# Sliding-window attention with sinks into a four-expert mixture: gates by token, first weights in pieces, score bursts joined

## The chip, the core and the metric

One core of one Trainium2 chip runs the whole kernel in one launch. The metric is device time in microseconds (us) of that core. TensorE (PE in the profile) has a matmul stream and a weight-load stream (PEld) beside it; VectorE (DVE), ScalarE (ACT), GpSimd (POOL) and SyncE (SP) have a queue of their own each. GpSimd and SyncE here issue nearly all DMAs. The inputs lie in DRAM in fp32; the load through GpSimd's DMA turns them into bf16 on the way.

## The reference

```python
# attention: q, k, v are (B, H, S, D) = (4, 8, 768, 64); 4 sink keys, window 128
scores = (q @ k.T) / sqrt(D)
keep   = (key_pos < 4) | ((0 <= q_pos - k_pos) & (q_pos - k_pos < 128))
a      = softmax(where(keep, scores, -1e9))
x      = (a @ v) with heads side by side            # (3072 tokens, 512)
# mixture: 4 experts, w1 (512, 1024), w2 (1024, 512)
p   = domain_probs / (domain_probs.sum(-1) + 1e-9)  # (3072, 4), the gates
out = sum over e of p[:, e] * (relu(x @ w1[e]) @ w2[e])
```

Every token goes through all four experts, so the mixture is by far the larger part of the arithmetic. The output is fp32, 3072 x 512.

## The kernel before

**Tiles.** Tokens are taken in twelve groups of 256, three to a batch: group (b, g). A unit (b, g, e) is the first product of one group with one expert. It leaves H = relu(x w1), as bf16, in two layouts: plain (eight blocks of 128 hidden columns) or as the parts that the second product needs.

**Attention, for each batch.** Rows of q and k are turned so that the 64 elements of a head lie on partitions: on TensorE for batch 0 (L579), by a transposing DMA in SyncE's queue for the batches after (L247). Then, for each of four head pairs and each group, scores of two heads are computed at once on 64 rows each (L685), ScalarE takes the exponential (L710), VectorE multiplies by the window's mask (L704, L719; for the first group of batch 0 a bias matmul, L679, takes its place), the four sink keys are treated beside that (L646, L654), the values are multiplied (L744, L751), VectorE takes the reciprocal of the row sums (L778) and the result is scaled (L781, L790). The result is turned to x by TensorE in batch 0 (L809) and by SyncE's transposing DMA after that (L768). A run of score matmuls between other matmuls is called a burst here: one head pair has six matmuls, and two head pairs in one burst have twelve. `Attention.options` (L849) says which steps could come next; `Attention.two` (L844) says whether the next two score steps may be joined.

**Mixture.** Units before `START[e]` are plain: eight blocks of four matmuls of 256 columns into a bank each (L1071). All others use a seven-product (Strassen-like) form on 2x2 blocks: products P1 to P7 (L1158) of forms of w1 (`weight_form1`, made on VectorE, L364 to L383) with forms of the tokens (L1127); ScalarE and VectorE add parts between banks (L1204, L1211, L1217, L1226), and VectorE applies relu and the gate together (L1191). The second products of the first two groups (`NEARLY`) are plain: eight matmuls of 512 columns into one of two banks `acc` (L1423), scaled by the gate `scale_t` and summed over the experts by VectorE (L1433, L1435), and stored (L1441). The ten other groups again use seven products, each summed over the four experts (L1335), copied out by ScalarE (L1375, L1397), added by VectorE (L1381, L1386) and stored by SyncE (L1324, L1383). These ten share one buffer `osb`.

**Gates.** The probabilities `dp` lie in SyncE's first loads as 24 rows of 128 tokens. They are needed in two ways. `gates_by_row` (L431) normalises them in this layout, writes them to DRAM, and `load_gate` (L452) loads one row to all partitions for the seven-product units. `gates` (L918), called just ahead of the first plain second product, turns `dp` on TensorE (four fp32 matmuls of 24 rows, L921), normalises on VectorE (L923 to L926) and leaves `scale_t`, 128 x 24 x 4, of which the plain second products use the first four tiles of 128 tokens.

**Loads.** GpSimd's queue loads q, k, v and the weights. `load_w1` (L308) loads w1 of an expert in `parts` pieces of columns; before the change expert 0 comes in two halves (L492, L493), the others in one piece, each w2 in one. The first loads stand in the code in order; the later ones come from a list `loads` (L1459 to L1461, extended in the main loop).

**What sets the order.** The instruction streams come from a planner that runs while the program is built. It keeps an estimated clock for each engine and DMA path (`t`, L103) and cost functions (`pe`, `act`, `dve`, `pool`, `sp`, `lands`), a ring of six PSUM banks, and a list of evictions to come (`later`, `flush`). At each turn of the main loop (L1481 to L1563) it collects what could be issued on TensorE next: steps of attention, a first product of an open unit, the opening of a new unit, a plain second product, one of the seven second products. Each has a ready time and a priority (`DUE`, `LOW_PRODUCT`, `OPEN` and so on; lower goes first). Among those ready within 40 ns the lowest priority number is taken, else the one ready first. Attention counts as due when it is behind its share of the mixture's work (`SHARE_OF`); a batch's attention may begin when the mixture has done a part (`LEAD`) of the work of the batches before. Where nothing is ready in the first 20 us by the planner's clock, `idle_products` (L555) issues matmuls on zeros. Weight forms are made when `form_due` and its counterpart for w1 say so (L388 to L398).

Of the kernel before, what the change touches and what calls it, by code (L numbers as in the profile page):

```python
# [10 lines left out]
AX = mybir.AxisListType  # L11
FP32 = mybir.dt.float32
# [4 lines left out]
def kernel(  # L17
# [12 lines left out]
    nc = tc.nc  # L30
# [7 lines left out]
    P = 128  # L38
# [22 lines left out]
    FIRST = 1  # L61
    START = {0: (1, 0), 1: (0, 2), 2: (0, 0), 3: (1, 0)}
    MIX = 6
    SHARE_OF = (0.91, 0.78, 1.08)
    LEAD = (1.01, 0.90)
    DUE = 1.5
    LOW_PRODUCT = 2.7
    LOW_SECOND = 2.7
    HIGH_PRODUCT = 1.9
    EARLY = -0.01  # L70
    MASK = 4000
    GATE = 1500
    GATE0 = 500
    FORM = 6000
    TOKEN = 5000
    MARGIN = 500
    HOLD = 0
    FULL = 7
    STEP0 = 0.01
    READY = 40  # L80
    WIDE = 2
    OPEN = 2.2
    SOON = 21000
    NEARLY = 2
    ROWED = 24000
    GATED = 38000
# [1 line left out]
    ROWS1 = 1500  # L88
    ONACT = 1
    ONE = 2  # L90
    PAIR = 1
    BEHIND = 1500
    CHORES = 3
    BIASED = 1
# [8 lines left out]
    t = {"pe": 1200.0, "act": 0.0, "dve": 0.0, "pool": 1280.0, "sp": 800.0, "sw": 6500.0, "hw": 0.0}  # L103
    ring, whole = [0.0] * 6, [False] * 6
    WARM = 6600.0
    FLIP, LATE, SLOW = 300, 2500, 1500

    def pe(cols, *deps, n=1, switch=0):
        t["pe"] = max([t["pe"], *deps])
        rate = 2.4 if t["pe"] > WARM else 1.2  # L110
        t["pe"] += cols / rate + 2.5 * n + 95 * switch
        return t["pe"] + 215
# [16 lines left out]
    def free_at(n=1):  # L129

        return sorted(ring)[n - 1]
# [51 lines left out]
        return act(cols) if engine == "act" else dve(cols, rate=rate, fixed=fixed)  # L183

    landed = {}
    ROW = {64: 12.8, 128: 22.6, 512: 79.8, 1024: 156.2}

    def lands(key, rows, cols, *deps):
        issued = pool(0, *deps, fixed=880)
# [118 lines left out]
    def load_w1(e, parts=1, which=None):  # L308
        if e not in w1_sb:
            w1_sb[e] = wpool.tile([P, NDB, F], BF16, name=f"w1_{e}", tag=f"w1_{e}")  # L310
        n = F // parts
        for i in which or range(parts):
            nc.gpsimd.dma_start(
                out=w1_sb[e][:, :, i * n:(i + 1) * n],
                in_=moe_w1[e][:, i * n:(i + 1) * n].rearrange("(db p) f -> p db f", p=P),
            )
# [71 lines left out]
    def form1_due(e):  # L388
        n = formed1.get(e, 0)
        if e == E - 2 and not (loaded and out_sb):  # L390
            return False
        return landed.get(("w1", e), 1e12) + 4000 < t["pe"] and (n < 3 or n == 3 and not left1[e])

    def form_due(e):
        n = formed.get(e, 0)
        if e == E - 1 and spared_at.get("w2", 1e12) > t["pe"]:
            return False
        return landed.get(("w2", e), 1e12) + 9000 < t["pe"] and (n < 3 or n == 3 and e in used)  # L398

    forming = []  # L400

# [94 lines left out]
    landed["w1", 0, 1] += 300  # L496
    landed["w1", 0] += 300
    load_w2(0)
    for base, sgn in ((0, 1), (NSINK - 1, -1)):
# [225 lines left out]
    def scores_ready(b, hp, g, n=1):  # L725
        return max([free_at(2 * n)] + [x for i in range(n) for x in turned(b, g, hp + i)])
# [98 lines left out]
    class Attention:  # L825
# [16 lines left out]
            return bool(self.todo or self.scored or self.valued)  # L842

        def two(self):  # L844
            return self.b >= PAIR and len(self.scored) <= 2 and len(self.todo) > 1 and self.todo[0][::3] == self.todo[1][::3] and self.todo[0][0] == "scores"

        def flip_ready(self):
            _, b, g, hp = self.flips[0]
# [3 lines left out]
        def options(self):  # L852

            if self.valued:
                yield turn_ready(*self.valued[0]), "turn"
            if self.scored and len(self.valued) < 3:
                yield values_ready(*self.scored[0]), "values"
            if self.todo:
                kind, b, x, y = self.todo[0]
                if kind == "scores":  # L860
                    if len(self.scored) < 4:
                        yield scores_ready(b, x, y), "todo"
                    if self.two():
                        yield scores_ready(b, x, y, 2), "two"
                elif kind == "keys":
                    yield max(turned(b, 0)), "todo"
                elif kind == "sinks":
                    nxt = self.todo[1] if len(self.todo) > 1 else None
                    if b >= 1 and nxt and nxt[0] == "scores":
                        if len(self.scored) < 4:  # L870
                            yield max(sinks_ready(b, x, y), scores_ready(*nxt[1:]), free_at(3)), "both"
                    else:
                        yield sinks_ready(b, x, y), "todo"
            if self.flips:
                yield self.flip_ready() + (FLIP if self.b == 0 and self.flips[0][2] else 0), "flip"
# [37 lines left out]
                    sink_values(b)  # L913


    scale_t = consts.tile([P, NT, E], FP32, name="scale_t")

    def gates():  # L918
        pt = acc[1][:, 0:E * NT].rearrange("p (e t) -> p e t", e=E)
        for e in range(E):  # L920
            nc.tensor.transpose(pt[:, e], dp[:, :, e], identf[0:NT, 0:NT])  # L921
# [4 lines left out]
        nc.vector.tensor_mul(  # L926
            scale_t, pt.rearrange("p e t -> p t e"), rs[:, :, None].to_broadcast([P, NT, E]),
        )
        acc_free[1] = dve(600, pe(400, acc_free[1]))

    NH = 6
    QF = NFB // 2
# [5 lines left out]
    class Mixture:  # L938
# [63 lines left out]
        def unit_ready(self, b, g, e, first):  # L1002
# [10 lines left out]
        def early_ready(self, g):  # L1013
            if not self.early[g] or not self.room():
                return 1e12
            return max(t["pe"], self.unit_ready(0, g, self.early[g][0], True))

        def firsts(self):

            early = sum(map(len, self.early.values()))  # L1020
            zero = sum(u["unit"] < PAIRS[0] for u in self.open)
            n = len(self.open)
            for i, u in enumerate(self.open):
                b, g, e = u["unit"]
                if u["fast"]:
                    for m in u["left"]:
                        yield max(u["at"].get(m, 1e12), free_at() if m == "P5" else 0.0), 2 + STEP0 * i, (u, m)
                else:
                    j = u["left"][0]
                    yield self.unit_ready(b, g, e, j < QF // 2), 2 + STEP0 * i, (u, j)  # L1030
            if n < WIDE and early:
                at, g = self.next_early()
                yield at, (OPEN if n else 2), ("early", g)
            if n < WIDE and self.units and (self.units[0][0] or loaded) and early <= MIX and self.room() and not (early + zero and self.live >= NH - 1):
                yield self.unit_ready(*self.units[0], False), (OPEN if n else 2) - EARLY, ("unit",)

        def emit_first(self, what, ready):

# [442 lines left out]
    while mix.more() or att.more():  # L1481
# [54 lines left out]
        opts += [(max(f, now), p, "first", x) for f, p, x in mix.firsts()]  # L1536
# [62 lines left out]
```

## Time and profile before

| | us |
|---|---|
| median of three timed runs | 359.38 (358.82, 359.38, 360.85) |
| the profiled execution's own time | 359.66 |
| its span in the trace | 358.0 |
| PE busy, matmuls | 351.3 |
| PEld busy, weight loads | 302.8 |
| DVE busy | 305.9 |
| ACT busy | 165.5 |
| POOL busy | 71.6 |

The span runs from the first to the last recorded instruction; the execution's own time has 1.66 us around it. Busy times of different engines overlap, and matmul ends are modelled, so a busy PE is not PE at its peak. The profile's page cuts the span into 40 equal slices and gives each engine's busy tenths in each:

```profile
PE   8999999999999999999998999999999999999996
DVE  6787979986999999798798899899889799899840
...
PEclk9999999999999999999999999999999999999999
DMA  9999999999999999617299812010220132111011
```

TensorE's line is at nine tenths or more except at both ends and in one slice of the middle; the granted clock is full throughout; the DMA engines are busy for the first 16 slices, in which q, k, v of the first batches, all weights and the first gates come in, and mostly idle later.

### The profile page before, as it was taken

How to read it: one execution, taken by the hardware profiler on the slowest of the kernel's cores; microseconds unless marked ns; L12 is line 12 of the kernel's file. 1: busy time of each engine (PE TensorE's matmuls, PEld its weight loads, DVE VectorE, ACT ScalarE, POOL GpSimd, SP SyncE). 2: the span in 40 equal slices, each digit the busy share in tenths (PEclk: the TensorE clock that was granted, in tenths of full speed). 3: DMA queues.
4: the chain of work that ended last, by engine and by line, in shares of the span. 5: the costliest groups of instructions: out<-in, count | busy, mean ns of one | idle time of the engine just before them, and what ended most of it. 6: DMA issues, size and time to landing. Idle time of an engine off the chain costs nothing.

```text
span 358.0 us, 10896 instructions
## 1 busy us (share of the span) xinstructions
PE 351.3 (98%) x4568; PEld 302.8 (85%) x4568; DVE 305.9 (85%) x698; ACT 165.5 (46%) x424; POOL 71.6 (20%) x92
## 2 busy tenths in 40 slices
PE   8999999999999999999998999999999999999996
PEld 4585769756789988989998898999899999999985
DVE  6787979986999999798798899899889799899840
ACT  5764623448782564556543445345444422313111
POOL 8945115230626106001061000000000000000000
PEclk9999999999999999999999999999999999999999
DMA  9999999999999999617299812010220132111011
GB/s 172 180 188 200 221 218 181 164 150 183 157 130 155 126 174 132 86 60 76 31 158 166 140 58 60 33 60 21 56 75 17 32 75 60 31 42 35 1 60 60
DMA packets 118013, 37.79 MB, mean 106 GB/s; under 512 B 100692, under 2 KB 113460, under 8 KB 117964
## 3 DMA queue, kind: packets, MB, share of 16 engines
q0 software_dynamic: 77520, 17.31, 56.5%
q1 hardware_dynamic: 39388, 19.28, 28.8%
q8 instruction: 35, 0.57, 0.7%
q10 hardware_dynamic: 1056, 0.52, 0.5%
q14 instruction: 14, 0.11, 0.1%
HBM read 40.98 MB, written 6.34 MB: 132 GB/s over the span
## 4 chain that ended last, share of the span: by engine, by line
PE 91%; DMA 4%; ACT 2%; POOL 1%; DVE 1%; issue 0%; SPq 0%; ACTq 0%
PE cps L1158 35%; PE acc L1335 33%; PE hps L1071 8%; PE acc L1423 7%; PE sps L685 3%; PE od L751 3%; DMA out_dram<-osb 2%; DMA qkn<-in_k_dram 2%; PE od L744 1%; ACT aT L710 1%; POOL qkn L235 1%; POOL vx L300 1%; PE tr L579 0%; DVE osb L1433 0%; PE tx L809 0%
## 5 line engine op out<-in xcount | busy, mean ns | idle before, releaser
L1158 PEld LDWEIGHTS <-w 128*128 128x128 bf16 x1280 | 78.5, 98 | 2.7 <-issue 1.3
L1335 PEld LDWEIGHTS <-H 128*128 128x128 bf16 x708 | 65.2, 98 | 7.5 <-issue 1.3
L1191 DVE SCALAR_TENSOR_TENSOR H<-cps,gates 128x512 bf16<-128x512 f32 x99 | 66.3, 681 | 1.5 <-PE cps L1158 1.3
L1158 PEld LDWEIGHTS <-vf 128*128 128x128 bf16 x960 | 58.6, 98 | 1.7 <-issue 0.8
L710 ACT ACTIVATE aT<-sps 128x512 bf16<-128x512 f32 (+1 forms) x96 | 47.6, 572 | 23.5 <-PE sps L685 23.4
L1335 PE MATMUL acc<-w,H 128*128 128x256 bf16 x420 | 55.4, 273 | 0.0
L1158 PE MATMUL cps<-T,w 128*128 128x128 bf16 x640 | 48.7, 219 | 0.0
L1158 PE MATMUL cps<-xT,w 128*128 128x128 bf16 x640 | 48.2, 219 | 0.0
L1158 PE MATMUL cps<-T,vf 128*128 128x128 bf16 x640 | 46.7, 219 | 0.0
L1204 ACT COPY cps<-cps 128x512 f32<-128x512 f32 x40 | 23.2, 581 | 44.1 <-PE cps L1158 32.7
L790 ACT ACTIVATE onat<-od,R 128x64 bf16<-128x64 f32 x144 | 33.5, 336 | 18.0 <-DVE R L778 18.0
L1211 DVE TENSOR_TENSOR cps<-H,cps 128x512 f32<-128x512 f32 x35 | 24.2, 691 | 12.5 <-PE cps L1158 10.6
L1335 PEld LDWEIGHTS <-S 128*128 128x128 bf16 x320 | 30.1, 98 | 4.6 <-issue 1.6
L1397 ACT COPY osb<-acc 128x256 f32<-128x256 f32 x35 | 13.1, 377 | 41.7 <-PE acc L1335 38.7
L300 POOL DMA_DIRECT2D vx<-in_v_dram x24 | 21.4, 897 | 53.5 <-PE od L751 43.0
L1071 PE MATMUL hps<-xT,w 128*128 128x256 bf16 x256 | 31.3, 273 | 0.0
L1423 PE MATMUL acc<-w,H 128*128 128x512 bf16 x128 | 30.1, 379 | 0.0
L1335 PE MATMUL acc<-wf,H 128*128 128x256 bf16 (+1 forms) x208 | 28.4, 272 | 0.0
L1071 PEld LDWEIGHTS <-w 128*128 128x128 bf16 x256 | 24.3, 98 | 4.2 <-issue 0.3
L1226 DVE TENSOR_TENSOR H<-H,cps 128x512 f32<-128x512 f32 x35 | 23.8, 681 | 2.8 <-PE cps L1158 2.6
L1158 PE MATMUL cps<-xT,vf 128*128 128x128 bf16 x320 | 24.4, 219 | 0.0
L704 DVE TENSOR_TENSOR aT<-aT,mask 128x1024 bf16<-128x1024 bf16 (+1 forms) x36 | 22.8, 637 | 1.3 <-ACT aT L710 1.2
(127 smaller groups left out, 516.7 us busy)
## 6 DMA issues: line engine op xcount, KB each, us to landing
w<-in_moe_w_dram POOLq DMA_DIRECT2D x7, 1024.0 KB, 16.8
out_dram<-osb SPq DMA_DIRECT2D x21, 256.0 KB
gates<-gate_rows SPq DMA_DIRECT2D x40, 128.0 KB
vx<-in_v_dram POOLq DMA_DIRECT2D x24, 128.0 KB, 6.7
qkn<-in_q_dram POOLq DMA_DIRECT2D x22, 128.0 KB, 8.0
qkn<-in_k_dram POOLq DMA_DIRECT2D x22, 128.0 KB, 10.5
w<-in_moe_w_dram POOLq DMA_DIRECT2D x2, 512.0 KB, 9.0
kraw<-in_k_dram ACTq DMA_DIRECT2D x2, 256.0 KB
```

The costliest lines, as they stand in the source:

```text
L300: nc.gpsimd.dma_start(out=vx[tb][:, :, 0:D], in_=v[b, :, tb * P:(tb + 1) * P, :].rearrange("h p d -> p h d"),)
L704: nc.vector.tensor_mul(a, a, m[:, None, :].to_broadcast([P, 2, w]))
L710: nc.scalar.activation(out=a[:, ph], in_=sps[ph][:, 0:w], func=AF.Exp, scale=scale)
L790: nc.scalar.mul(o[:, qi, hp, ph * D:(ph + 1) * D], od[:, qi, ph, 0:D], R[:, qi, ph])
L1071: nc.tensor.matmul(h[:, i].rearrange("p (q n) -> p q n", q=2), lhsT=w1_sb[e][:, db, fb * P:(fb + 1) * P], rhs=xT[b, g][:, :, db], start=(i ...
L1158: nc.tensor.matmul(y[:, f], lhsT=A[:, d, f * P:(f + 1) * P], rhs=T[:, d], start=(m in ("P1", "P5") and f == 0 and d == 0), stop=(d == 1), ...
L1191: nc.vector.scalar_tensor_tensor(out=dst, in0=src, scalar=0.0, in1=gate, op0=ALU.max, op1=ALU.mult)
L1204: nc.scalar.copy(out=tiles["Y"], in_=y)
L1211: nc.vector.tensor_add(tiles["V"], c5, tiles["X"])
L1226: nc.vector.tensor_add(c5, c5, y)
L1335: nc.tensor.matmul(y, lhsT=self.operand(b, g, e, m)[:, f], rhs=forms[e][m][:, f, cs], start=(k == 0 and f == 0 and m in (("P1", "P5", "P2" ...
L1423: nc.tensor.matmul(op, lhsT=H[:, fb // QF, fb % QF, s], rhs=w2_sb[e][:, fb, :], start=(fb == 0), stop=(fb == NFB - 1),)
```

## The change

**Gates by token.** `scale_t` is now 128 x 4 x 4 and is loaded by a DMA of SyncE, tokens on partitions, right after the loads of the sink values; a piece of it is four fp32 numbers. `gates` only normalises it in place on VectorE: no matmuls, and the first plain second product does not wait for the bank that they used.

**First weights in pieces.** w1 of expert 0 is loaded by four DMAs of 256 columns instead of two of 512, w1 of expert 1 by two instead of one. `unit_ready` looks up the landing of the piece that a product uses, where it knew the first half and the whole before. The planner's assumed landings change with that.

**Single bursts wait for joined ones.** Where the next two score steps could be joined, the single one is now called "one" instead of "todo" and gets a priority number of at least `DUE + ALONE`, unless attention is late by more than `OVER` steps or the batch is the first. While a joined burst is possible, due and not late, and at least `HOLDS` units are open, `joins` keeps new units from being opened. With `PAIR = 0` joined bursts are allowed in batch 0, too.

**Order refitted.** Twelve of the planner's constants have other values, so that the order changes from the start to the end of every queue.

```diff
-    SHARE_OF = (0.91, 0.78, 1.08)
-    LEAD = (1.01, 0.90)
-    DUE = 1.5
-    LOW_PRODUCT = 2.7
+    SHARE_OF = (0.9, 0.79, 0.98)
+    LEAD = (1.01, 1.0)
+    DUE = 1.9
+    LOW_PRODUCT = 2.3
...
-    GATE0 = 500
+    GATE0 = 900
...
-    MARGIN = 500
+    MARGIN = 0
...
-    SOON = 21000
+    SOON = 34000
...
-    PAIR = 1
+    HOLDS = 1
+    MORE = 2
+    BOTH = 1
+    PAIR = 0
+    OVER = 4
+    ALONE = 1.3
...
-    FLIP, LATE, SLOW = 300, 2500, 1500
+    FLIP, LATE, SLOW = 500, 2900, 1500
...
-        return landed.get(("w1", e), 1e12) + 4000 < t["pe"] and (n < 3 or n == 3 and not left1[e])
+        return landed.get(("w1", e), 1e12) + 3000 < t["pe"] and (n < 3 or n == 3 and not left1[e])
...
-        return landed.get(("w2", e), 1e12) + 9000 < t["pe"] and (n < 3 or n == 3 and e in used)
+        return landed.get(("w2", e), 1e12) + 14000 < t["pe"] and (n < 3 or n == 3 and e in used)
...
+    scale_t = consts.tile([P, 2 * NEARLY, E], FP32, name="scale_t")
+    nc.sync.dma_start(out=scale_t, in_=moe_domain_probs[0:2 * NEARLY * P].rearrange("(t p) e -> p t e", p=P))
...
-    load_w1(0, 2, [0])
-    load_w1(0, 2, [1])
+    load_w1(0, 4, [0])
+    load_w1(0, 4, [1])
+    load_w1(0, 4, [2])
+    load_w1(0, 4, [3])
...
-                        yield scores_ready(b, x, y), "todo"
+                        yield scores_ready(b, x, y), "one" if self.two() else "todo"
...
-        pt = acc[1][:, 0:E * NT].rearrange("p (e t) -> p e t", e=E)
-        for e in range(E):
-            nc.tensor.transpose(pt[:, e], dp[:, :, e], identf[0:NT, 0:NT])
-        rs = consts.tile([P, NT], FP32, name="rs")
-        nc.vector.reduce_sum(out=rs, in_=pt.rearrange("p e t -> p t e"), axis=AX.X)
+        rs = consts.tile([P, 2 * NEARLY], FP32, name="rs")
+        nc.vector.reduce_sum(out=rs, in_=scale_t, axis=AX.X)
...
-            return max(free_at(), landed.get(("w1", e, 0), 1e12) if first else landed.get(("w1", e), 1e12), *xs)
+            return max(free_at(), landed.get(("w1", e, (j // 2, j)[e == 0]), landed.get(("w1", e), 1e12)), *xs)
...
-                    ready = max(ready, acc_free[self.turn % 2])
...
-        loads += [(load_w1, e), (load_w2, e)]
+        loads += [(load_w1, e, 2) if e in (1,) else (load_w1, e), (load_w2, e)]
...
-            opts = [(max(r, now), (DUE if due else 3) - 0.1 * (step == "two"), "att", step) for r, step in att.options()]
+            late = ahead == 0 or (att.steps + OVER) * share <= (mix.done - upto) * att.total
+            for r, step in att.options():
+                p = (DUE if due else 3) - 0.1 * (step == "two")
+                if step == "one" and not late:
+                    p = max(p, DUE + ALONE)
+                opts.append((max(r, now), p, "att", step))
...
+        joins = due and ahead >= PAIR and att.two() and not late and len(mix.open) >= HOLDS
+        opts += [(max(f, now), p, "first", x) for f, p, x in mix.firsts() if not (joins and x[0] in ("unit", "early"))]
```

More of the change, by code (lines that the diff above doesn't have):

```diff
@@ L185 @@
     landed = {}
-    ROW = {64: 12.8, 128: 22.6, 512: 79.8, 1024: 156.2}
+    ROW = {64: 12.8, 128: 22.6, 256: 41.7, 512: 79.8, 1024: 156.2}
     def lands(key, rows, cols, *deps):
@@ L491 @@
     load_v(0, (2, 3))
-    load_w1(0, 2, [0])
-    load_w1(0, 2, [1])
+    load_w1(0, 4, [0])
+    load_w1(0, 4, [1])
+    load_w1(0, 4, [2])
+    load_w1(0, 4, [3])
     t["sw"] += 1300
     landed["w1", 0, 0] += 700
-    landed["w1", 0, 1] += 300
+    landed["w1", 0, 1] += 500
+    landed["w1", 0, 2] += 300
+    landed["w1", 0, 3] += 300
     landed["w1", 0] += 300
@@ L844, in two @@
         def two(self):
-            return self.b >= PAIR and len(self.scored) <= 2 and len(self.todo) > 1 and self.todo[0][::3] == self.todo[1][::3] and self.todo[0][0] == "scores"
+            return self.b >= PAIR and len(self.scored) <= MORE and len(self.todo) > 1 and self.todo[0][::3] == self.todo[1][::3] and self.todo[0][0] == "scores"
         def flip_ready(self):
@@ L868, in options @@
                     nxt = self.todo[1] if len(self.todo) > 1 else None
-                    if b >= 1 and nxt and nxt[0] == "scores":
+                    if b >= BOTH and nxt and nxt[0] == "scores":
                         if len(self.scored) < 4:
@@ L913, in emit @@
                     sink_values(b)
-    scale_t = consts.tile([P, NT, E], FP32, name="scale_t")
     def gates():
-        pt = acc[1][:, 0:E * NT].rearrange("p (e t) -> p e t", e=E)
-        for e in range(E):
-            nc.tensor.transpose(pt[:, e], dp[:, :, e], identf[0:NT, 0:NT])
-        rs = consts.tile([P, NT], FP32, name="rs")
-        nc.vector.reduce_sum(out=rs, in_=pt.rearrange("p e t -> p t e"), axis=AX.X)
+        rs = consts.tile([P, 2 * NEARLY], FP32, name="rs")
+        nc.vector.reduce_sum(out=rs, in_=scale_t, axis=AX.X)
         nc.vector.tensor_scalar_add(out=rs, in0=rs, scalar1=1e-9)
         nc.vector.reciprocal(out=rs, in_=rs)
[L926 to L929, printed above, removed]
+        nc.vector.tensor_mul(scale_t, scale_t, rs[:, :, None].to_broadcast([P, 2 * NEARLY, E]))
+        dve(200)
     NH = 6
@@ L1000, in opened, with unit_ready @@
             return {"unit": (b, g, e), "fast": fast, "left": list(UNITS) if fast else list(range(QF)), "at": {}}
-        def unit_ready(self, b, g, e, first):
+        def unit_ready(self, b, g, e, j):
             xs = [xT_at.get((b, hp, g), 1e12) for hp in range(NHP)]
@@ L1015, in early_ready @@
                 return 1e12
-            return max(t["pe"], self.unit_ready(0, g, self.early[g][0], True))
+            return max(t["pe"], self.unit_ready(0, g, self.early[g][0], 0))
         def firsts(self):
@@ L1029, in firsts @@
                     j = u["left"][0]
-                    yield self.unit_ready(b, g, e, j < QF // 2), 2 + STEP0 * i, (u, j)
+                    yield self.unit_ready(b, g, e, j), 2 + STEP0 * i, (u, j)
             if n < WIDE and early:
@@ L1034, in firsts @@
             if n < WIDE and self.units and (self.units[0][0] or loaded) and early <= MIX and self.room() and not (early + zero and self.live >= NH - 1):
-                yield self.unit_ready(*self.units[0], False), (OPEN if n else 2) - EARLY, ("unit",)
+                yield self.unit_ready(*self.units[0], QF), (OPEN if n else 2) - EARLY, ("unit",)
         def emit_first(self, what, ready):
@@ L1535 @@
         opts.append((max(p, now), HIGH_PRODUCT if behind > BEHIND or mix.live >= FULL else LOW_PRODUCT, "product", None))
-        opts += [(max(f, now), p, "first", x) for f, p, x in mix.firsts()]
+        joins = due and ahead >= PAIR and att.two() and not late and len(mix.open) >= HOLDS
+        opts += [(max(f, now), p, "first", x) for f, p, x in mix.firsts() if not (joins and x[0] in ("unit", "early"))]
         opts.append((max(s2, now), 1 if mix.since >= 1 else LOW_SECOND, "second", None))
```

## The prediction, made before the changed kernel ran

> **What bounds the kernel now.** I read the page first, then TensorE's waits, then stretches of the span, and last the timeline where a stretch has idle time. The page's head:
>
> ```profile
> span 358.0 us, 10896 instructions
> ...
> PE 351.3 (98%) x4568; PEld 302.8 (85%) x4568; DVE 305.9 (85%) x698; ACT 165.5 (46%) x424; POOL 71.6 (20%) x92
> ...
> PE 91%; DMA 4%; ACT 2%; POOL 1%; DVE 1%; issue 0%; SPq 0%; ACTq 0%
> ...
> L1335 PE MATMUL acc<-w,H 128*128 128x256 bf16 x420 | 55.4, 273 | 0.0
> ```
>
> PE is busy for 351.3 of 358.0 us, and 91% of the chain that ended last is PE. So two things alone change the time: what the PE stream contains, and the few places where it stands still. Those are named by the view of waits, TensorE's own (us in total, times, longest):
>
> ```profile
> PE acc L558 <- DVE lent L469: 1.4, 1, 1.4
> PE acc L1335 <- ACT osb L1397: 0.9, 1, 0.9
> PE tr L579 <- DMA qkn<-in_k_dram: 0.2, 1, 0.2
> PE tx L809 <- DVE onat L781: 0.2, 1, 0.2
> ```
>
> The first is the launch and stays; the last two are in the first 22 us; the second is the one wait of the long middle, and the stretch around it is the first row below. The second row is where VectorE is the next bound (columns: stretch, length, busy PE, PEld, DVE, ACT, POOL, clock, DMA, GB/s):
>
> ```profile
> 192.00:196.00 4.00, 3.07 (x40) 2.72 (x38) 2.98 (x8) 0.75 (x3) 0.07 (x1) 1.00 1.78 210
> 90.00:140.00 50.00, 50.00 (x723) 44.84 (x722) 48.83 (x119) 30.13 (x91) 21.79 (x27) 1.00 1.63 143
> ```
>
> The granted clock is 1.00 in both, so cycles saved are time saved. The profiled execution took 359.66 us, 1.66 around its span; the median of the three timed runs is 359.38, 0.28 lower. I sum against 359.66 and carry the difference to 359.38. A measurement of this kernel can tell about 0.5%, that is 1.8 us, from no change.
>
> **Part 1: score bursts.** A score matmul uses 64 rows, two at a time, everything else mostly 128. A burst of one head pair and a burst of two, in PE's timeline:
>
> ```profile
> 157.14 0.60 PE L1335 MATMUL acc<-w,H 128*128 128x256 bf16 x4
> 157.68 0.40 PE L685 MATMUL sps<-qkT 64*128 64x128 bf16 x6
> 158.00 1.05 PE L1335 MATMUL acc<-w,H 128*128 128x256 bf16 x8
> ...
> 162.34 0.60 PE L1335 MATMUL acc<-w,H 128*128 128x256 bf16 x4
> 162.87 0.62 PE L685 MATMUL sps<-qkT 64*128 64x128 bf16 x12
> 163.42 0.62 PE L1158 MATMUL cps<-T,w 128*128 128x128 bf16 x8
> ...
> 192.39 0.60 PE L1335 MATMUL acc<-wf,S 128*128 128x256 bf16 x4
> 192.83 0.60 PE L1335 MATMUL acc<-qkn,S 128*128 128x256 bf16 x4
> ```
>
> Four products take 0.44 (192.39 to 192.83). So the single burst with its two changes of mode costs 158.00 - 157.14 - 0.44 = 0.42, the joined one 163.42 - 162.34 - 0.44 = 0.64, against 0.84 for two singles: joining saves **0.20**. I counted unbroken runs of score matmuls in the instruction orders of both kernels, batch by batch: 10, 10, 9, 9 before and 10, 9, 7, 7 after. That is five bursts fewer, **-1.0**. The part that the change's words put first in batch 0 (joining allowed there) has no effect on the count: 10 and 10.
>
> A rule that would price this otherwise: the Trainium skill, "TensorEngine Tiling (Array Packing)", Key Properties, says that changing the tiling mode drains the array, and "TensorE: Matmul & The Clock Gate", Single matmul latency, puts a warm matmul at (398 + columns)/2.4 ns, a constant of 166 ns beyond streaming. The trace agrees with the latency (273 ns for 256 columns in the row above). An estimate from these pages with a full drain at both ends would be 0.33 a burst and -1.7 for five; the rows above measure less, and I keep them.
>
> **Part 2: gates, idle products, one seed.** PE's timeline around the gates' transposes and around some idle products, and a piece of the chain (start, us, what):
>
> ```profile
> 26.65 0.65 PE L921 MATMUL acc<-scratch 24*128 24x24 f32 x4
> 27.24 2.33 PE L1423 MATMUL acc<-w,H 128*128 128x512 bf16 x10
> ...
> 12.57 0.49 PE L558 MATMUL acc<-lent 128*128 128x256 bf16 x3
> 12.89 0.33 PE L579 MATMUL tr<-ident,qkn 128*128 128x128 bf16 x3
> ...
> 31.76 1.74 PE acc L1423 x8
> ```
>
> The four transposes leave the stream: 27.24 - 26.65, **-0.6**. VectorE's four steps on the gates stay, on a smaller tile. The new order has 26 idle products of 256 columns or more for 28, each 0.32/3: **-0.2**. One first product now finds its second bank not wholly written and adds a 512-column matmul, 1.74/8: **+0.2**. Every other class of matmul has the same count in both orders. So the stream is 1.0 + 0.6 + 0.2 - 0.2 = **1.6 us** shorter. This much is certain if the rows hold; the rest is waiting.
>
> **Part 3: the start.** GpSimd issues two DMAs more (w1 of expert 0 in four), ahead of the mask of sink values, the sink keys and the next loads; SP issues one more, 512 pieces of 16 bytes (128 partitions by 4).
>
> ```profile
> 8.96 1.54 POOL L313 DMA_DIRECT2D w<-in_moe_w_dram  x2
> 10.43 0.95 POOL L323 DMA_DIRECT2D w<-in_moe_w_dram  x1
> 12.84 0.67 POOL L609 TENSOR_TENSOR ksd<-qkT,half 128x8 bf16<-128x8 bf16 x4
> 13.40 0.45 PE L579 MATMUL tr<-ident,qkn 128*128 128x128 bf16 x5 [0.17 <-DMA qkn<-in_k_dram]
> 15.16 0.43 PE L646 MATMUL sinks<-qkT,ksd 128*32 128x256 bf16 x4
> 15.53 0.68 PE L685 MATMUL sps<-qkT 64*128 64x128 bf16 x6
> ...
> DMA to landing us min/median/max: 14.6/14.6/14.6
> ...
> DMA to landing us min/median/max: 15.5/15.5/15.5
> ...
> 43.21 1.89 PE L1423 MATMUL acc<-w,H 128*128 128x512 bf16 x8
> ...
> q0 software_dynamic: 77520, 17.31, 56.5%
> ```
>
> GpSimd runs without a gap here, so the sink keys of 12.84 to 13.51 move by 1.54 to 15.05, and up to 0.4 more if the fourth quarter or w2 has to wait for a DMA counter. TensorE's sinks at 15.16 therefore wait up to 0.4; behind them stands the burst of 15.53, which takes 0.68 where one elsewhere takes 0.40, so 0.28 of that is covered by a wait that exists already. The 512 pieces cost between nothing and, at q0's mean of 0.565 x 16 x 358.0 / 77520 = 0.042 us over 16 engines, 1.3 us of the loads' time. If the key load that ends TensorE's wait at 13.40 lands 0.2 to 0.4 later, the two idle products moved in front of it and the late sink keys cover most. On the other side the new order puts a first w1 product at about 16.5 where two idle products and a gap stood. I take **0** for the start, from -0.5 to +0.9.
>
> Two weights are needed earlier. w2 of expert 0, issued at 10.43, lands 14.6 later at 25.0; it was used at 27.24 and would be wanted at about 26.3. w2 of expert 1 (the 15.5, issued at 25.3) lands at 40.8; used at 43.21, now with 1.2 us less matmul work ahead, wanted at 42.0. So each has some 1.2 us of cover, less than the 1.3 above only at its end: **0**, at worst +0.5.
>
> The Trainium skill speaks against this part: "DMA: Bandwidth & Descriptors", Queues, rings and completion order, says that each DMA engine takes turns between queues packet by packet, and its Specifications that pieces under 512 bytes lose line rate, so SP's small load would delay GpSimd's big ones rather than slip beside them. By its 10.5 ns a packet (section Bandwidth) the estimate is 32 x 10.5 ns = 0.3 us, inside the range taken from rows; no run here shows such a load yet.
>
> **Part 4: the wait at 193.** SP's queue, ScalarE and TensorE:
>
> ```profile
> 175.59 0.40 PE L685 MATMUL sps<-qkT 64*128 64x128 bf16 x6
> 178.95 3.23 SPq L247 DMA_TRANSPOSE qkT<-qkn  x2
> 182.75 0.37 ACT L1397 COPY osb<-acc 128x256 f32<-128x256 f32 x1 [1.63 <-PE acc L1335]
> 185.74 0.59 SPq L1324 DMA_DIRECT2D out_dram<-osb  x1
> 193.94 0.65 ACT L1397 COPY osb<-acc 128x256 f32<-128x256 f32 x2 [1.84 <-DMA out_dram<-osb]
> 194.36 1.03 PE L1335 MATMUL acc<-w,S 128*128 128x256 bf16 x8 [0.93 <-ACT osb L1397]
> ```
>
> The result of 182.75 is stored from the only buffer; the store starts 3 us late behind transposes of batch 3, lands at 193.9, and only then may the next group's results be copied out. TensorE stops from 192.83 + 0.44 to 194.36: 1.1. What lets those transposes start is the last score burst of batch 2 at 175.59. In the new order, its matmuls summed with the durations of these rows, that burst is a joined one and stands 13.8 us before the same copy instead of 7.2, so the transposes should be through before the store. I take **-1.1**; the bounds are -1.1 and +1.0, the latter if the store is as late, because the same sum finds 1.0 us less work than before between the two results.
>
> **Part 5: VectorE from 90 to 140.** It is busy 48.83 of 50, and its work there is the same after the change, while TensorE arrives about 1 us earlier and has some three bursts, 0.6, less to do. If VectorE cannot go faster, that comes back as waits for VectorE's adds and gated results. Bounds 0 (1.17 us are free) and 1.6; I take **+0.6**. Over the whole span it has 52 us free, so I cost the moved weight forms and priorities elsewhere at nothing: TensorE's work hides them, and if one step is late, that shows once, with 305.9/698 = 0.44 us on average.
>
> **Sum:** -1.6 + 0 - 1.1 + 0.6 = **-2.1**. The profiled execution's 359.66 becomes 357.6, the median's 359.38 becomes **357.3**.
>
> **Rivals.**
> *More comes through.* VectorE keeps pace (0 for +0.6) and the start gains its 0.5: 357.3 - 1.1 = 356.2. For it: after the launch no row of TensorE's waits names VectorE for more than 0.2. Against: 48.83 of 50.
> *The waits come back.* VectorE takes its full 1.6, or the store's wait stays: 358.3 to 358.4, both 359.4. For it: joined bursts ask for four of six banks and two masks at once, in a stage with no free VectorE. Against: the joined bursts of before (162.87) have no wait beside them. Here the change does what it says and shows little.
> *Slower: the loads become the bound up to 42 us.* Place: w2 of expert 1. The DMA engines work through one backlog, so a delay of the start stays to the end of the loads, and each us beyond the cover of 1.2 is a us of TensorE. It undoes the 2.1 from a delay of 3.3 on, and passes +1.8 from 5.1. Price at 5.3, four times what I bound for the 512 pieces: 361.4. Against: that bound.
>
> **How the numbers follow.** Forecast 0.50, its own range 356.5 to 358.0; more comes through 0.17; waits come back 0.23; slower 0.10. 0.5% below 359.38 is 357.58. Of the forecast about 0.35 lies under it, with nearly all of the first rival: faster 0.54. Slower by over 0.5% is 0.09 of the last. The rest, 0.37, is within. The range 355.9 to 359.4 leaves out the last rival and about 0.05 of each end of the others.
>
> **What would show it.** Right: no L921 row and 27.24's group right behind the first products; 33 bursts; the wait on ACT's copy in the 192 to 196 stretch gone; TensorE's first w1 product before 17. Wrong: sinks waiting for GpSimd by over 0.5; TensorE waits on VectorE in 90 to 140 of over 1.6 in total; a wait for w2 near 26 or 42; a new wait for the output store.

## The result and the profile after

The changed kernel takes **357.18 us** (median of seven runs, 356.84 to 357.87); the kernel before, timed beside it, 359.57 (seven runs, 358.82 to 361.16). The ratio is 0.993, 95% interval 0.9908 to 0.9952: 2.4 us less, faster by 0.5% to 0.9%. The forecast was 357.3.

The page's head after, with the lines that answer to those of before. The code has moved: L685 of before is L696, L1335 is L1339, L1397 is L1401, L1423 is L1426, L1071 is L1075, L1127 is L1131; the edits of the experiments shift them by a few lines again.

```profile
span 355.7 us, 10876 instructions
...
PE 349.3 (98%) x4563; PEld 302.4 (85%) x4563; DVE 305.8 (86%) x699; ACT 165.0 (46%) x423; POOL 74.1 (21%) x95
```

TensorE's waits in the changed kernel (us in total, times, longest):

```profile
PE acc L569 <- DVE lent L474: 1.4, 1, 1.4
PE acc L1339 <- ACT osb L1401: 0.5, 1, 0.5
PE sinks L657 <- POOL ksd L620: 0.2, 1, 0.2
PE tx L820 <- DVE onat L792: 0.2, 1, 0.2
```

TensorE is busy 2.0 us less, of 2.3 us less span, and VectorE as long as before: the gain is mostly work that left the matmul stream. The wait on the output buffer, which I had expected to go, is still there, at half its length. The start of the plain second products and the wait, in TensorE's timeline:

```profile
22.57 3.87 PE L1075 MATMUL hps<-xT,w 128*128 128x256 bf16 x32
26.27 4.05 PE L1426 MATMUL acc<-w,H 128*128 128x512 bf16 x18
```

```profile
190.70 0.60 PE L1339 MATMUL acc<-qkn,S 128*128 128x256 bf16 x4
191.77 0.60 PE L1339 MATMUL acc<-w,S 128*128 128x256 bf16 x4 [0.47 <-ACT osb L1401]
```

No transposes stand in front of the products of 26.27; before, these began at 27.24. The stop at 191 is 191.77 - 190.70 - 0.44 = 0.63, against 1.1 before. Of the four signs of being right that the prediction named, three are in this profile: no transposes of the gates, 33 score bursts for 38, and a first w1 product before 17 (at 16.21, for 18.30 before). The fourth, that the wait on ScalarE's copy is gone, is not.

### The profile page after: what moved, and what is told of

Its sections match the earlier page's. It is cut to its first block, busy times and chain, and to the rows that moved or that the text cites. A ratio compares the mean times of both kernels' runs of the same rounds, so it can differ in the third digit from the quotient of the medians.

```text
span 355.7 us, 10876 instructions
## 1 busy us (share of the span) xinstructions
PE 349.3 (98%) x4563; PEld 302.4 (85%) x4563; DVE 305.8 (86%) x699; ACT 165.0 (46%) x423; POOL 74.1 (21%) x95
## 4 chain that ended last, share of the span: by engine, by line
PE 95%; DVE 3%; ACT 1%; issue 0%; ACTq 0%; DVEq 0%
PE cps L1162 36%; PE acc L1339 34%; PE acc L1426 8%; PE hps L1075 7%; PE sps L696 3%; PE od L762 3%; PE acc L569 1%; DVE aT L730 1%; PE od L755 1%; DVE onat L792 1%; PE tx L820 0%; PE sinks L657 0%; PE tr L590 0%; DVE T L1131 0%; ACT qkT L276 0%; ACT aT L721 0%
## 5 line engine op out<-in xcount | busy, mean ns | idle before, releaser
L1339 PEld LDWEIGHTS <-H 128*128 128x128 bf16 x684 | 63.5, 98 | 7.3 <-issue 1.1
L1195 DVE SCALAR_TENSOR_TENSOR H<-cps,gates 128x512 bf16<-128x512 f32 x96 | 64.2, 680 | 0.1
L1339 PE MATMUL acc<-w,H 128*128 128x256 bf16 x408 | 53.9, 273 | 0.0
L1401 ACT COPY osb<-acc 128x256 f32<-128x256 f32 x35 | 13.1, 376 | 50.9 <-PE acc L1339 50.9
L1339 PEld LDWEIGHTS <-S 128*128 128x128 bf16 x320 | 30.1, 98 | 4.3 <-issue 1.1
L1075 PE MATMUL hps<-xT,w 128*128 128x256 bf16 x256 | 31.8, 273 | 0.1
L1426 PE MATMUL acc<-w,H 128*128 128x512 bf16 x128 | 29.9, 379 | 0.0
L1339 PE MATMUL acc<-wf,H 128*128 128x256 bf16 (+1 forms) x208 | 28.4, 272 | 0.0
L1075 PEld LDWEIGHTS <-w 128*128 128x128 bf16 x256 | 24.2, 98 | 4.6 <-issue 0.9
L240 POOL DMA_DIRECT2D qkn<-in_q_dram x22 | 19.7, 893 | 22.5 <-DMA qkT<-qkn 14.6
```

The lines of the kernel that those rows point to most:

```text
L240: nc.gpsimd.dma_start(out=both[:, i], in_=src[b, :, tb * P:(tb + 1) * P, :].rearrange("h p d -> p h d"),)
L1075: nc.tensor.matmul(h[:, i].rearrange("p (q n) -> p q n", q=2), lhsT=w1_sb[e][:, db, fb * P:(fb + 1) * P], rhs=xT[b, g][:, :, db], start=(i ...
L1195: nc.vector.scalar_tensor_tensor(out=dst, in0=src, scalar=0.0, in1=gate, op0=ALU.max, op1=ALU.mult)
L1339: nc.tensor.matmul(y, lhsT=self.operand(b, g, e, m)[:, f], rhs=forms[e][m][:, f, cs], start=(k == 0 and f == 0 and m in (("P1", "P5", "P2" ...
L1426: nc.tensor.matmul(op, lhsT=H[:, fb // QF, fb % QF, s], rhs=w2_sb[e][:, fb, :], start=(fb == 0), stop=(fb == NFB - 1),)
```

## The experiments

The runs below take the terms of the prediction's sum one by one. The reference for each is the kernel before, timed beside it (median of 23 runs); since that median differs from one set of runs to the next (358.9 to 359.54), ratios are compared, not times. A ratio need not equal the quotient of the two medians.

**The gates alone, on the kernel before.**

```diff
+    scale_t = consts.tile([P, 2 * NEARLY, E], FP32, name="scale_t")
+    nc.sync.dma_start(out=scale_t, in_=moe_domain_probs[0:2 * NEARLY * P].rearrange("(t p) e -> p t e", p=P))
...
-        pt = acc[1][:, 0:E * NT].rearrange("p (e t) -> p e t", e=E)
-        for e in range(E):
-            nc.tensor.transpose(pt[:, e], dp[:, :, e], identf[0:NT, 0:NT])
...
```

> The kernel before with one part of the change alone: scale_t loaded by token and normalised in place, no turning on TensorE; every other instruction stands in the order of before. My sum (four transposes leave the stream, 27.24 - 26.65): 0.6 us faster than before, some 359.0, and the row of the plain second products starts right behind the first products. Rival, the loads pay for it: the 512 pieces delay w1 and w2 of expert 0 by up to 1.3 us, and TensorE waits for w2 near 26: no faster or up to 0.7 slower. Rival, nothing comes through since the time is given back at the store's wait near 193: 0.0.

Measured: 359.22, before 359.5, ratio 0.9985 (0.9964 to 1.0006): -0.5 by the ratio, -0.3 by the medians, with an interval that includes 0. The plain second products start earlier in its timeline:

```profile
25.79 0.82 PE L1066 MATMUL hps<-xT,w 128*128 128x256 bf16 x6
26.44 1.89 PE L1418 MATMUL acc<-w,H 128*128 128x512 bf16 x7
```

That is 0.8 earlier than before, 0.6 of it the transposes. The loads do not pay: w2 of expert 0 landed at 24.6 (25.0 before). And the profile showed what I had not looked for: no wait at 193, but one of 1.7 us at 113.6 for VectorE (below).

**Splitting the joined bursts.**

```diff
+        if more == 1 and not biased:
+            nc.tensor.matmul(sps[0][:, 0:P], lhsT=ident, rhs=ident, start=True, stop=True, skip_group_check=True)
         c = 0
         for (kb, qb, nq) in GROUPS[g]:
```

> The changed kernel, with a matmul of 128 columns on 128 rows put between the two halves of 12 joined score bursts (its result is overwritten); nothing else moves. My pricing of a joined burst (0.42 for a single, 0.64 for a joined one) gives 0.20 a burst for the two further changes of mode, and 0.05 for the matmul: 12 x 0.25 = 3.0 us slower than the changed kernel, some 360.2. The pricing by a full drain at both ends (0.33) gives 12 x 0.38 = 4.6 us, some 361.8. If joining saved nothing, 12 x 0.05 = 0.6 us, some 357.8.

Measured: 361.1, ratio 1.0039 (1.0025 to 1.0054), span 359.3, which is 3.6 longer than the changed kernel's. The same burst in TensorE's timeline, of the changed kernel and of the one with the split:

```profile
164.14 0.60 PE L1339 MATMUL acc<-wf,S 128*128 128x256 bf16 x4
164.67 0.61 PE L696 MATMUL sps<-qkT 64*128 64x128 bf16 x12
165.22 1.05 PE L1339 MATMUL acc<-wf,S 128*128 128x256 bf16 x8
```

```profile
165.08 0.60 PE L1341 MATMUL acc<-wf,S 128*128 128x256 bf16 x4
165.61 0.39 PE L698 MATMUL sps<-qkT 64*128 64x128 bf16 x6
165.94 0.23 PE L693 MATMUL sps<-ident 128*128 128x128 bf16 x1
166.10 0.40 PE L698 MATMUL sps<-qkT 64*128 64x128 bf16 x6
166.43 1.05 PE L1341 MATMUL acc<-wf,S 128*128 128x256 bf16 x8
```

From start to start, less 0.44 for the four products: 0.64 joined, 0.91 split. The two changes of mode and a matmul of 0.05 cost 0.27, so the changes 0.22; 12 x 0.27 = 3.2. Of the 3.6 in the span, 2.7 lie before the last four matmuls (at 354.63 for 351.93), and 0.9 behind them, where the last two stores take 2.17 us to issue for 1.23; that end has no burst in it. The price of 0.20 stands, and the full drain (0.38 with the matmul, 4.6 in sum) does not.

**The store from ScalarE's queue.**

```diff
-                nc.sync.dma_start(out=out[r + P:r + 2 * P, c], in_=out_sb[b, g][1][:, c])
+                (nc.sync if final else nc.scalar).dma_start(out=out[r + P:r + 2 * P, c], in_=out_sb[b, g][1][:, c])
```

> The changed kernel, with the store of the second 128 tokens of a group issued from ScalarE's queue, right behind ScalarE's own copy, and not from SyncE's, in nine of the ten groups; the order on TensorE is the same. Theory: the wait left in the changed kernel at 191.03 (0.63) is the output buffer that waits for a store queued behind SyncE's transposes (ready at about 182.0, issued at 184.63): it goes, 0.5 to 0.7 us faster than the changed kernel, some 356.6. Rival: the landing takes as long as before because the transfer itself is slow beside the transposes (6.6 us from issue): 0 to 0.2 faster. Rival on the other side: the issue holds ScalarE some 0.5 us in each group, and TensorE waits for ScalarE's copies: up to 1 us slower.

Measured: 357.03, ratio 0.9919 (0.99 to 0.9938), not told apart from the changed kernel. SyncE's queue in the changed kernel, then ScalarE's in this one:

```profile
179.50 1.24 SPq L779 DMA_TRANSPOSE xT<-onat  x1
180.84 2.21 SPq L252 DMA_TRANSPOSE qkT<-qkn  x1
183.14 1.40 SPq L463 DMA_DIRECT2D gates<-gate_rows  x1
184.63 0.57 SPq L1328 DMA_DIRECT2D out_dram<-osb  x1
```

```profile
182.00 0.34 ACTq L1328 DMA_DIRECT2D out_dram<-osb  x1
...
191.82 0.65 ACT L1401 COPY osb<-acc 128x256 f32<-128x256 f32 x2 [5.43 <-DMA out_dram<-osb]
```

The store is issued at 182.00 and not at 184.63, and the copy that waits for it still starts at 191.8 (191.34 in the changed kernel). The chain of waits gives the landing, here and in a second profile of the changed kernel:

```profile
182.00 9.46 DMA out_dram<-osb
```

```profile
184.61 7.23 DMA out_dram<-osb
```

Issued 2.6 us earlier, the store landed at 191.5 for 191.8. So in this execution the place in SyncE's queue, on which my part 4 rested, did not set the landing, and the first rival holds. It is one profile, of the slowest of the six runs (356.19 to 357.67); the times can't exclude a gain of some tenths in the others.

**Output buffer in two halves, on both kernels.**

```diff
-                    x2 = mo.tile([P, 2, Dout], FP32, name="osb", tag="osb", bufs=1)
-                    out_sb[b, g] = [x2[:, i] for i in range(2)]
+                    out_sb[b, g] = [mo.tile([P, Dout], FP32, name=f"osb{i}", tag=f"osb{i}", bufs=1) for i in range(2)]
```

> The changed kernel, with the output buffer of a group as two buffers, one for each 128 tokens, in the same space; the order on every engine is the same. Theory: the wait left at 191.03 is the first copy into the upper half, held by the store of the lower half of the group before, which shares the buffer with it. It now waits for the store of the upper half alone, which was issued some 10 us earlier: the wait goes, 0.4 to 0.6 us faster than the changed kernel, some 356.6. Rival: the first copy into the lower half follows so soon that the wait only moves there: 0 to 0.2 faster. Rival: the time is given back behind it, where another wait had been hidden: 0.

> The kernel before, with the output buffer in two halves in the same way and nothing else. Theory: the wait at 193.16 costs 1.1 us there, so this is 1.1 faster than before, some 358.4; and this is the whole of what any part of the change could have had from that wait. Rival: the wait is as long only in some executions (a run of the kernel before with the gates alone had none there), so that its mean price is 0.5 or less: some 359.0.

On the changed kernel: 356.62, ratio 0.9926 (0.99 to 0.9952), and TensorE's waits and its stretch at 191 are these:

```profile
PE acc L569 <- DVE lent L474: 1.4, 1, 1.4
PE tx L820 <- DVE onat L792: 0.2, 1, 0.2
```

```profile
190.00:194.00 4.00, 4.00 (x59) 3.81 (x57) 2.98 (x9) 1.45 (x3) 0.00 (x0) 1.00 0.79 136
```

TensorE is busy for all of the 4 us: the first copies of a group waited for the store of the other half only because the two shared a buffer. (Nine of the ten groups share it; one of the last batch has its result in tiles of `aT`.) The wait is in seven of the eight profiles of the changed kernel and its variants with the one buffer, and in neither of the two with halves. On the kernel before: 358.97 beside 358.9, ratio 0.9993 (0.9976 to 1.001). There the wait was not worth 1.1; the rival holds, and the next pair of runs shows why.

Neither kernel with halves stops for the buffer, so the pair also shows what the rest of the change is worth: 358.97 and 356.62 side by side, with spans of 357.2 and 354.8. The first plain second product and the last matmuls, without the change and with it:

```profile
27.55 3.63 PE L1423 MATMUL acc<-w,H 128*128 128x512 bf16 x16
...
353.34 0.39 PE L1335 MATMUL rest<-qkn,H 128*128 128x128 bf16 x4
```

```profile
26.20 5.34 PE L1426 MATMUL acc<-w,H 128*128 128x512 bf16 x24
...
351.05 0.39 PE L1339 MATMUL rest<-qkn,qkT 128*128 128x128 bf16 x4
```

Of the 2.4, 1.35 lie before the first of these rows, 0.94 between the two (325.79 and 324.85), and 0.1 behind.

**Both kernels once more, for second profiles.**

> The kernel before, once more, for a second profile of it. Its times so far lie mostly from 358.6 to 359.4 with a tail to 361.1. Theory: the wait at 193.16 (1.1) is of the tail: a profile whose own time is below 359.2 shows none or below 0.4 there, one of 359.5 and more shows about 1 or another wait for a transposing DMA. Then my 1.1 was not in the typical time of before, and its going cannot be in the difference of the medians. Rival: the wait is there in every execution, also in one of 358.7, and the tail has other causes.

> The changed kernel, once more, for a second profile and for its time on the chip of the runs beside it. 0.7% faster than before, some 357.0. Theory: its wait at 191 too varies from execution to execution between 0 and 0.7.

Before again: 359.96 beside 359.54, from 358.62 to 362.01; the changed kernel 357.53, ratio 0.9931 (0.9907 to 0.9955). TensorE's waits in the new profile of the kernel before (its own time 360.27), a piece of its chain of waits, and the changed kernel's waits in its new profile (357.9):

```profile
PE acc L558 <- DVE lent L469: 1.4, 1, 1.4
PE cps L1158 <- DVE cps L1211: 1.3, 1, 1.3
```

```profile
107.63 6.87 DMA xT<-onat
114.50 0.02 issue
114.52 0.30 DVE T L1127
...
115.54 0.62 DVE cps L1211
116.16 0.04 issue
116.20 0.61 PE cps L1158 x8
```

```profile
PE acc L1339 <- ACT osb L1401: 1.2, 1, 1.2
```

In this execution of the kernel before the wait at 193 is absent, although its time is above 359.5; in its place a transposing DMA for x, issued at 107.6, takes 6.9 us to land, VectorE makes the forms of the tokens late, and TensorE stops for 1.4 us before the product of 116.20. That is the second half of the theory (another wait for a transposing DMA), seen with the gates alone as well. TensorE then comes to the place of the wait at 193 some 1.7 us later (the same products at 194.51 for 192.83), so this profile can't tell whether the store landed any sooner; that the wait is not in the typical time of before rests on the run with the buffer in halves. In the changed kernel the wait at 191 is 1.3 here and 0.63 in the first profile. So these waits come and go with the landing of DMAs from execution to execution. Less its wait each execution comes to about the same: 359.66 - 1.1 = 358.6 and 360.27 - 1.4 = 358.9 before, 357.61 - 0.6 = 357.0 and 357.9 - 1.3 = 356.6 after. The difference of these, about 2, is what does not depend on them; the pair with halves, which has none of them, gave 2.4.

**More work for VectorE.** Two doses of the same edit (the second kernel has `b == 1 and g and hp == 1`):

```diff
                     nc.vector.tensor_mul(a, a, m[:, None, :].to_broadcast([P, 2, w]))
+                    if b == 1 and g:
+                        nc.vector.tensor_mul(a, a, m[:, None, :].to_broadcast([P, 2, w]))
```

> The changed kernel, with the mask's multiplication done twice in eight score steps of batch 1 (the second has no effect on the values): 8 x 0.60 = 4.8 us more for VectorE between 88 and 110. If VectorE bounds the stretch from 90 to 140, as my 0.6 of a loss there supposed (0.94 us are idle in the changed kernel): +3 to +4 us, some 360.7. Rival: VectorE's queue is full but TensorE has other work in hand for the time that VectorE is late, and VectorE catches up behind 140: below +1 us, some 357.6.

> The changed kernel, with the mask's multiplication done twice in two score steps of batch 1, 2 x 0.60 = 1.2 us more for VectorE between 88 and 110; eight such steps, 4.8 us, had cost 5.4. If VectorE bounds the stretch throughout, 5.4/4.8 x 1.2 = 1.35 us slower than the changed kernel, some 358.5. If VectorE can be about 1 us late before TensorE waits, which would be why the 1.5 us that TensorE gained ahead of it did not come back as waits: 0 to 0.4, some 357.3.

Measured: eight steps 362.62, ratio 1.0077 (1.0058 to 1.0096), against the changed kernel's 0.993 some 5.3 us; two steps 358.05, ratio 0.9972 (0.9957 to 0.9987), some 1.5. TensorE's wait for the masked scores with eight steps and with two:

```profile
PE od L764 <- DVE aT L717: 3.4, 7, 1.0
```

```profile
PE od L764 <- DVE aT L717: 0.3, 1, 0.3
```

The large dose comes through in full, and from 90 to 140 VectorE is now busy for 49.65 of the 50 us, TensorE for 46.46: VectorE bounds this stretch for work that stands between a score and its value product. The small one came out at about its full price by time, with an interval of some 0.3% either way that does not reach 0, though only 0.3 of it is in this wait; that VectorE has 1 us in hand for such work is not borne out. My belief in the bound was right; the loss that I drew from it was not, since the changed kernel has no such wait at all.

**The first w1 in halves.**

```diff
-            nc.gpsimd.dma_start(
-                out=w1_sb[e][:, :, i * n:(i + 1) * n],
+            if e or i % 2 == 0:
+                m = n if e else 2 * n
+                nc.gpsimd.dma_start(
+                    out=w1_sb[e][:, :, i * n:i * n + m],
...
```

> The changed kernel, with w1 of expert 0 loaded in two halves at the places of the first and third quarter; the order on TensorE is the same. My prediction gave the start nothing in sum. By the landings (first quarter 15.61, first half some 16.8) the first product of 16.21 waits 0.6 us, while the sink keys come 1.5 earlier on GpSimd and save TensorE's wait of 0.2: 0.4 us slower than the changed kernel, some 357.6, with a wait of TensorE for w1 near 16.3. Rival: the idle time in front of it moves and all is hidden by 27: 0. Rival: the two issues saved bring the later loads forward: 0.2 faster.

Measured: 356.86, ratio 0.9934 (0.991 to 0.9958), by time not told apart from the changed kernel. Its start in TensorE's timeline:

```profile
17.05 1.05 PE L1077 MATMUL hps<-xT,w 128*128 128x256 bf16 x8 [0.90 <-DMA w<-in_moe_w_dram]
...
26.68 1.67 PE L1428 MATMUL acc<-w,H 128*128 128x512 bf16 x7
```

The first product waits 0.9 for w1, and the plain second products come at 26.68 for 26.27: the quarters are worth the 0.4 that was expected at this place. It is one profile, though, and near the scatter: the nine profiles of kernels with quarters have 26.19 to 26.48 there. The wait at 191 happens to be absent in this one, so the loss does not show in the time.

**Without the rule that single bursts wait.**

```diff
-                        yield scores_ready(b, x, y), "one" if self.two() else "todo"
+                        yield scores_ready(b, x, y), "todo"
...
-        joins = due and ahead >= PAIR and att.two() and not late and len(mix.open) >= HOLDS
+        joins = False
```

> The changed kernel without the rule that single bursts wait for joined ones (a single burst has its old priority, and no unit is held back); the planner sets a new order from about 90 us on. It has 36 score bursts for 33 and one seed matmul less: 3 x 0.20 - 0.22 = 0.4 us slower than the changed kernel by my prices, some 357.4. If a joined burst in the stretch where VectorE is full brings waits of its own, the kernel without the rule is no slower or up to 0.5 faster.

Measured: 358.48, ratio 0.9962 (0.9942 to 0.9982), beside 357.53 for the changed kernel in the same call. Its profile's span is 356.8 with a wait of 1.2 at 191, that of the changed kernel there 356.2 with the same wait: 0.6 for three bursts more, near the 0.4 expected; 0.2 of it lies before the first plain second product, where the two kernels have the same order. The medians, 0.95 apart, include waits that vary.

**Halves, and w2 behind the sink keys.** The halves as above, and the DMA of w2 of expert 0 is issued behind the sink values, not from its place behind w1:

```diff
...
             run("pool")
+            issue_w2(0)
```

> The changed kernel with the output buffer in two halves, and w2 of expert 0 issued by GpSimd behind the sink keys and sink values of batch 0 and not ahead of them. The sink keys come 0.9 us earlier, so TensorE's wait for them at 14.84 (0.21, in another run 0.5) goes; w2 is issued at some 15.5 for 12.2, while the queue still has w1 to bring until 19.6, and lands as before at 24.9. Theory: 0.2 us faster than the halves alone, some 356.4 on a chip where before takes 358.9. Rival: w2 lands later than 26.3 and TensorE waits for it: up to 1 us slower.

Measured: **356.49**, all six runs within 356.40 and 356.64, ratio 0.9904 (0.9882 to 0.9926); the changed kernel in the same call had 356.6 to 358.03. TensorE's waits are the launch and one of 0.2. The span is that of the halves alone, 354.8, so the move of w2 shows nothing by itself. That the halves take out what varied fits both kernels that have them; it was not timed beside the halves alone.

## Why the prediction was right, and where it was not

That the time came within 0.1 us of the forecast is in part luck. The stream's -1.6 was right; the two other terms, -1.1 and +0.6, were both wrong, in opposite ways, and the start and the waits that vary made up the 0.5 that was left of them. Parts of both main rivals came true: VectorE kept pace and the start gained, as in the first, and the store's wait stayed, as in the second.

- **Score bursts, -1.0: right.** 0.64 for a joined one, 0.42 for a single one in the changed kernel's timeline too; split again they cost 0.22. The stretch behind the start, 0.94 shorter in the pair with halves, holds these five bursts less the matmul of 512 columns that was added (+0.2). The estimate from the Trainium skill, "TensorE: Matmul & The Clock Gate", Single matmul latency (0.33 for both changes), is more than this case measures (0.20 to 0.22).
- **Gates, idle products, one seed, -0.6: right by the stream.** (The seed is that matmul of 512 columns.) With the gates alone the transposes' place closes up; the timed gain of 0.5 agrees, with an interval too wide to prove it.
- **The start, 0: a little better, within its range.** From 27.24 before, the stream alone gives 27.24 - 0.6 - 0.2 = 26.44; measured 26.27, a gain of 0.2. But 27.24 is the earliest of three profiles with the start of before; from the 27.48 and 27.55 of the others the gain is 0.4 to 0.5, which is what the quarters of w1 seemed worth. The wait for the sink keys came (0.2), w2 of expert 0 was no later, and the 512 pieces delayed nothing that can be seen (the estimate from the Trainium skill, "DMA: Bandwidth & Descriptors", section Bandwidth, had been 0.3). The landings, by DMAs of the one line, in the changed kernel:

```profile
L328 POOL DMA_DIRECT2D w<-in_moe_w_dram x1: 888/888/888, 12.2 to 12.2; - x1
...
DMA to landing us min/median/max: 12.7/12.7/12.7
```

12.2 + 12.7 = 24.9, for 25.0 before.

- **The wait at 193, -1.1: wrong.** The step that failed is "the transposes should be through before the store": in the changed kernel two transposes and a load of gates still stood ahead of it, and with the store issued from another queue the landing came no earlier, in the one profile taken. Also, one execution of before was taken for all: the wait is 1.1 in one profile and absent in the next. Between the two first profiles the term was -0.5; on the typical time of before its price is about 0, and the changed kernel has the wait in most profiles.
- **VectorE, +0.6: wrong.** The failed step is "its work there is the same after the change, while TensorE arrives about 1 us earlier". VectorE arrives earlier too. Its row of 44 to 90 before, and after (columns as in the prediction):

```profile
44.00:90.00 46.00, 46.00 (x455) 32.65 (x453) 38.75 (x70) 20.65 (x51) 12.27 (x14) 1.00 1.64 181
```

```profile
44.00:90.00 46.00, 45.90 (x462) 32.66 (x460) 40.21 (x75) 20.99 (x52) 12.23 (x14) 1.00 1.68 181
90.00:140.00 50.00, 50.00 (x731) 44.82 (x729) 49.06 (x120) 32.24 (x94) 22.53 (x27) 1.00 1.58 147
```

It did 1.5 us more before 90, where it had idle time, and 0.2 more in the stretch. So the lead was TensorE's and VectorE's together. Whether earlier input or the weight forms' new due times moved that work was not tried apart.

The sum of the two first profiles: -1.6 stream, -0.2 start, -0.5 wait, 0 VectorE: -2.3, as 358.0 to 355.7. The medians differ by 2.4, with a different share of waits on each side.

## What to carry to other kernels

Where one engine is busy 98% of the span, price a change by what leaves that engine's stream, from start to start in its timeline: those terms held to about 0.2 us. A wait that hangs on a DMA's landing should be seen in a second profile before it enters a sum. And when a new output waits for the store of an old one, look whether they only share a buffer: two buffers of half the size, in the same space, removed the wait, and the twelve runs with them lie from 356.40 to 357.02, where thirteen of the changed kernel lie from 356.6 to 358.03.

## What was not expected of the hardware

An output store of 256 KB issued 2.6 us earlier from a second queue landed no earlier to speak of (191.5 for 191.8; the copy behind it at 191.8 for 191.9 and 191.3). What held it, most likely GpSimd's loads and SyncE's transposes of the last batch, which move at the same time, was only argued. And a transposing DMA needed 6.9 us to land in an execution in which TensorE then waited 1.4 us for it, while in the first profile of the same kernel VectorE works on that tile at 112.4 without a wait, 5.6 us after the issue at 106.8.
